# Attention and a gated MoE layer on one core: three units in turn over halves of DFF, masked scores kept in PSUM, every queue ordered by a table

## The chip, the cores and the metric

The program runs on one NeuronCore of a Trainium2 chip. Its engines are TensorE (PE, matmuls; its weight loads are listed apart as PEld), VectorE (DVE), ScalarE (ACT), GpSimd (POOL) and SyncE (SP, which here only issues transfers). Each works through its own queue in order and waits on semaphores of the others. The metric is device time in microseconds. Three runs of the kernel before took 527.41, 528.01 and 529.1 us; the median is 528.01.

## What is computed

Eight sequences of 576 positions go through attention with 8 heads of 64 and a causal window of 64, and then through a layer with a convolution and a gate:

```python
scores = scale * np.matmul(q, k.transpose(0, 1, 3, 2))
mask = (rel >= 0) & (rel < window)                     # rel = query - key, window = 64
scores = np.where(mask, scores, -1000000000.0)
scores = scores - np.max(scores, axis=-1, keepdims=True)
attn = np.exp(scores)
attn = attn / (np.sum(attn, axis=-1, keepdims=True) + 1e-09)
x = np.matmul(attn, v)                                 # heads side by side: 512 columns
h = np.maximum(x @ w_in, 0.0)                          # w_in: 512 x 1024
conv_out[:, t] = sum(conv_w[k] * h[:, t + k - 1] for k in range(3))   # along the sequence
gate = 1.0 / (1.0 + np.exp(-conv_out))
out = h * gate @ w_out                                 # w_out: 1024 x 512
```

q, k and v are float32. The weights (w_in, conv_w, w_out) are float64 arrays, and reach the chip as pairs of 32-bit words.

## The kernel before

**Units.** The 8 x 576 positions are cut into NU = 12 units of NX = 384 positions, six blocks of 64 each. For every unit the kernel does an attention part and a MoE part.

**Attention of a unit.** Keys, queries and values are loaded (load_qk, load_v). Scores come in NBU = 3 bursts of NB = 4 blocks (qk, L357), into two PSUM banks. row_max (L364) adds the mask, scales, writes the masked scores to SBUF tiles `s` and leaves each row's extreme in `nm`. exps (L374) takes the exponentials from SBUF to SBUF with row sums. guard (L377), reciprocal (L380) and normalise (L385) follow. For the first two units (`wide`, BY_PE = 2) PE transposes the result (transpose_pe, L391) and untile copies it into `ub` (L396); for the others DVE transposes 32 x 32 blocks (L412) into `T`, and SP places them by twelve transfers a group (place, L424). values (L488) multiplies with V; split_hi (L492) and split_lo (L495) cut the result into two parts for fp32r matmuls.

**MoE of a unit.** For each f of NF = 8 blocks of 128 DFF columns mm1 (L508) does 12 matmuls of 128 x 384: 4 chunks of 128 rows times 3 products (high x high, low x high, high x low). relu (L525, L529) writes `hbuf`. For each pair of f: conv_mid on ACT (L535), conv_side twice per f on DVE (L542), sigmoid (L549), gate (L554), gate_hi (L558), gate_lo (L562). mm2 (L571) then does 3 matmuls for each of 4 output chunks, which add up over the 8 f in four PSUM banks `po`. The results are copied out (L607, L609) and stored.

**Weights.** Each weight block is loaded as raw 64-bit words into one of two buffers (`bits`), which share their memory with `T` and the result tile `ot`. to_f32 turns the words into float32 (L252 on ACT, L253 on POOL, L254 and L256 on DVE, L259 on ACT, L260 on DVE), then the high part (L275 or L277) and the low part (L278) are cut off.

**PSUM.** Eight banks: two for scores (`sc`), two for mm1 and values (`acc`), four for mm2 (`po`). Unit 0's second and third burst borrow `po`.

**Order.** All work is entered with a due time (`at`), many of them from the table START. `queued` plays the queues through with estimated costs and writes out an order by due time among what is ready; the tiles' semaphores then hold the engines to the data. Up to a set time PE's holes are filled with matmuls on a spare tile (keep_busy, L216). Units run one after another: unit u+1's attention values and unit u+2's scores lie among unit u's matmuls.

Of the kernel before, what the change touches and what calls it, by code (L numbers as in the profile page):

```python
# [46 lines left out]

class Work:


    def __init__(self, t, eng, cost, do, r, w, kind, mb, port):
        self.t, self.eng, self.cost, self.do, self.r, self.w, self.kind, self.mb = t, eng, cost, do, r, w, kind, mb
        self.port = port
        self.needs, self.after, self.ready = 0, [], 0.0
        self.start = self.end_ = 0.0


def queued(works, fill=None):

    import heapq
    writer, readers = {}, {}
    for x in works:
        deps = set()
        for k in x.r:
            if k in writer:  # L70
                deps.add(writer[k])
        for k in x.w:
            deps.update(readers.get(k, ()))
            if k in writer:
                deps.add(writer[k])
        deps.discard(x)
        for d in deps:
            d.after.append(x)
        x.needs = len(deps)
        for k in x.w:  # L80
            writer[k], readers[k] = x, []
        for k in x.r:
            readers.setdefault(k, []).append(x)
    free = {"PE": 0.0, "DVE": 0.0, "ACT": 2.0, "POOL": 0.7, "SP": 1.3}
    state = dict.fromkeys(free)
    waiting = {e: [] for e in free}
    touched = {k: ("", 0.0) for k in [("sc", 0)] + [("acc", i) for i in range(2)] + [("po", i) for i in range(NC)]}
    for x in works:
        if x.needs == 0:
            waiting[x.eng].append(x)  # L90
    dma, port, order, left = 0.0, {"DVE": 0.0, "POOL": 0.0}, [], len(works)
    while left:
        best = None
        for e, ws in waiting.items():
            if not ws:
                continue
            start = max(free[e], min(x.ready for x in ws))
            if best is None or start < best[0]:
                best = (start, e)
        start, e = best  # L100
        x = min((x for x in waiting[e] if x.ready <= start),
                key=lambda x: x.t - (0.5 if x.kind and x.kind == state[e] else 0.0))
        if x.port:
            if e == "POOL" and start < port["DVE"]:
                free[e] = port["DVE"]
                continue
            start = max(start, port["POOL"])
            port[e] = start + x.port
        waiting[e].remove(x)
        if fill and e == "PE" and start < FILL_TO:  # L110
            t = max(free[e], FILL_FROM)
            n = int((start - t) * FILL)

            clean = [(end, k) for k, (by, end) in touched.items() if by != "PE" and end < t]
            if n > 0 and clean:
                order.append(Work(x.t, e, 0.0, fill(n, min(clean)[1]), [], [], None, 0, 0.0))
        turn = SWITCH[e] if e in SWITCH and (x.kind != state[e] if e == "PE" else x.kind and x.kind != state[e]) else 0.0
        if turn and e == "PE" and not x.kind:
# [19 lines left out]
START = {  # L140
    "v0": -34.213,
    "pv0": -15.486,
    "conv": -34.622,
    "bits": ((-44.162, -48.108), (-49.962, -46.523)),
    "qk1": -44.058,
    "v1": -6.318,
    "qk2": 0.918,
    "qk0": (-88.698, -55.197, -55.435),
    "ex0": (-38.484, -35.539, -25.91),
    "sc1": (-35.664, -14.916, -14.661),  # L150
    "ex1": (-10.948, -3.722, -2.234),
    "mask": -13.894,
    "sig": ((5.143, 6.743, 8.637, 10.624), (2.954, 4.077, 7.59, 9.996), (4.046, 6.806, 8.285, 10.314)),
    "in": (-40.063, -38.679, -33.327, -12.569, -5.818),
    "out": (-5.241, -4.847, 7.996, 9.148),
# [13 lines left out]
def attention_moe(ctx: ExitStack, tc: tile.TileContext, q, k, v, w_in, conv_w, w_out, out):  # L169
# [56 lines left out]
    def two(t, eng, cost, do, **kw):  # L226
        at(t, eng, cost, do, port=cost, **kw)
# [74 lines left out]

    def wide(u):
# [429 lines left out]
```

## Time and profile before

| | |
|---|---|
| runs | 527.41, 528.01, 529.1 us |
| span of the profiled execution, first to last instruction | 528.6 us |
| busy: PE, DVE, ACT, POOL | 507.8, 377.7, 384.5, 105.5 us |
| mean granted TensorE clock | 0.994 |
| read from HBM, written | 47.73 MB, 9.47 MB |

The profile gives no other total of the profiled execution than its span, which lies between the lowest and the highest run. A row of a stage table is: stretch, its length, busy time (and instructions) of each engine, granted clock, DMA share, GB/s; taken for one line of the kernel it shows PE and PEld alone. A row of the timeline is: start, length, engine, line, operation, output<-input, shapes, count, and in brackets the idle time before it and what ended that. A row of the groups is: line, engine, operation, shapes, count, then busy time and mean nanoseconds of one, then the idle time before. Matmuls overlap each other, so their pace is read from the distance of their starts.

### The profile page before, as it was taken

How to read it: one execution, taken by the hardware profiler on the slowest of the kernel's cores; microseconds unless marked ns; L12 is line 12 of the kernel's file. 1: busy time of each engine (PE TensorE's matmuls, PEld its weight loads, DVE VectorE, ACT ScalarE, POOL GpSimd, SP SyncE). 2: the span in 40 equal slices, each digit the busy share in tenths (PEclk: the TensorE clock that was granted, in tenths of full speed). 3: DMA queues.
4: the chain of work that ended last, by engine and by line, in shares of the span. 5: the costliest groups of instructions: out<-in, count | busy, mean ns of one | idle time of the engine just before them, and what ended most of it. 6: DMA issues, size and time to landing. Idle time of an engine off the chain costs nothing.

```text
span 528.6 us, 14478 instructions
## 1 busy us (share of the span) xinstructions
PE 507.8 (96%) x5646; PEld 486.1 (92%) x5646; DVE 377.7 (71%) x1084; ACT 384.5 (73%) x1017; POOL 105.5 (20%) x192
## 2 busy tenths in 40 slices
PE   6867899999999999999999999999999999999996
PEld 4657799999899999999999999999999999999996
DVE  3998999998668676667767767767767767655552
ACT  1988999788795994696696697687687687544541
POOL 5663645112011120011021021021021021000000
PEclk9998999999999999999999999999999999999999
DMA  8982670265472264172173073083073053010011
GB/s 275 378 276 101 231 258 2 51 203 190 115 269 68 66 206 129 56 275 69 40 288 77 22 256 112 23 287 97 14 279 99 24 165 95 13 61 1 1 61 60
DMA packets 29459, 69.94 MB, mean 132 GB/s; under 512 B 5712, under 2 KB 17616, under 8 KB 29392
## 3 DMA queue, kind: packets, MB, share of 16 engines
q1 hardware_dynamic: 29392, 69.03, 39.6%
q8 instruction: 44, 0.72, 0.6%
q14 instruction: 23, 0.19, 0.1%
HBM read 47.73 MB, written 9.47 MB: 108 GB/s over the span
## 4 chain that ended last, share of the span: by engine, by line
PE 89%; DMA 4%; ACT 3%; DVE 2%; issue 1%; SPq 0%; ACTq 0%
PE po L571 39%; PE acc L508 38%; PE acc L488 6%; PE sc L357 5%; DMA q<-in_q_dram 2%; DMA T<-in_w_in_dram 1%; DVE s L364 1%; ACT ub L396 1%; ACT s L374 0%; ACT w L252 0%; DVE wil L278 0%; DVE w L260 0%; DVE xl L495 0%; DVE s L385 0%; ACT L374 0%
## 5 line engine op out<-in xcount | busy, mean ns | idle before, releaser
L508 PE MATMUL acc<-xh,wih 128*128 128x384 f32 x384 | 132.2, 344 | 1.8 <-ACT hbuf L529 0.9
L542 DVE SCALAR_TENSOR_TENSOR c<-hbuf,cw,c 128x386 f32<-128x386 f32 (+1 forms) x192 | 110.0, 624 | 32.8 <-ACT c L535 32.7
L571 PE MATMUL po<-gh,woh 128*128 128x386 f32 (+1 forms) x384 | 132.3, 345 | 0.0
L508 PE MATMUL acc<-xh,wil 128*128 128x384 f32 x384 | 130.9, 341 | 0.0
L508 PE MATMUL acc<-xl,wih 128*128 128x384 f32 x384 | 130.6, 340 | 0.0
L571 PE MATMUL po<-gh,wol 128*128 128x386 f32 (+1 forms) x384 | 129.8, 338 | 0.0
L571 PE MATMUL po<-gl,woh 128*128 128x386 f32 (+1 forms) x384 | 129.8, 338 | 0.0
L374 ACT ACTIVATE s<-s,nm 128x96 f32<-128x96 f32 (+2 forms) x288 | 105.4, 370 | 5.1 <-DVE nm L364 4.9
L508 PEld LDWEIGHTS acc<-xh,wih 128*128 128x128 f32 x384 | 72.9, 190 | 3.5 <-issue 2.1
L562 DVE TENSOR_TENSOR gl<-c,gh 128x772 fp32r<-128x772 f32 (+1 forms) x48 | 54.9, 1144 | 28.6 <-ACT gh L558 28.3
L571 PEld LDWEIGHTS po<-gh,woh 128*128 128x128 f32 x384 | 72.2, 188 | 2.9
L508 PEld LDWEIGHTS acc<-xl,wih 128*128 128x128 f32 x384 | 73.0, 190 | 0.0
L508 PEld LDWEIGHTS acc<-xh,wil 128*128 128x128 f32 x384 | 72.9, 190 | 0.0
L385 POOL TENSOR_TENSOR s<-s,r 128x768 f32<-128x768 f32 x27 | 39.7, 1471 | 165.4 <-DVE r L380 154.1
L554 DVE TENSOR_TENSOR c<-c,hbuf 128x772 f32<-128x772 f32 (+1 forms) x48 | 47.0, 980 | 36.0 <-ACT c L549 35.9
L571 PEld LDWEIGHTS po<-gl,woh 128*128 128x128 f32 x384 | 72.3, 188 | 0.0
L571 PEld LDWEIGHTS po<-gh,wol 128*128 128x128 f32 x384 | 72.3, 188 | 0.0
L529 ACT ACTIVATE hbuf<-acc 128x384 f32<-128x384 f32 x64 | 30.8, 484 | 46.2 <-PE acc L508 45.9
L549 ACT ACTIVATE c<-c 128x772 f32<-128x772 f32 (+1 forms) x48 | 40.7, 848 | 27.4 <-DVE c L542 27.2
L364 DVE CUSTOM_DVE_ANT_0 s<-sc,mask 128x96 f32<-128x96 f32 (+2 forms) x272 | 51.6, 254 | 9.0 <-POOL mask L328 5.3
L374 ACT ACTIVATION_READ_ACCUMULATOR s<-s,nm 128x1 f32 x288 | 55.2, 192 | 0.0
L535 ACT ACTIVATE c<-hbuf,cw 128x386 f32<-128x386 f32 (+1 forms) x96 | 53.6, 609 | 0.0
(64 smaller groups left out, 576.2 us busy)
## 6 DMA issues: line engine op xcount, KB each, us to landing
v<-in_v_dram SPq DMA_DIRECT2D x24, 768.0 KB, 7.1
ub<-T SPq DMA_DIRECT2D x240, 48.0 KB, 2.0
k<-in_k_dram SPq DMA_DIRECT2D x22, 448.0 KB, 5.6
q<-in_q_dram SPq DMA_DIRECT2D x22, 384.0 KB, 5.8
out_dram<-T SPq DMA_DIRECT2D x8, 772.0 KB, 4.4
T<-in_w_in_dram SPq DMA_DIRECT2D x8, 512.0 KB, 6.9
T<-in_w_out_dram SPq DMA_DIRECT2D x8, 512.0 KB, 5.1
out_dram<-T SPq DMA_DIRECT2D x3, 768.0 KB, 6.2
```

The costliest lines, as they stand in the source:

```text
L364: nc.vector.tensor_tensor_reduce(out=ss[b][:, i, h, o:n], in0=banks_of(u, b)[h][:, i * P + o:i * P + n], in1=mask[m][:, o:n], scale=-0.125 ...
L374: nc.scalar.activation(x, x, AF.Exp, bias=nms[b][:, e], scale=-1.0, accum_out=sms[b][:, e])
L385: on.tensor_tensor(sv, sv, rs[b].unsqueeze(2).broadcast_to([P, 2 * NB, n]), ALU.mult)
L488: nc.tensor.matmul(acc[bank(("v", u, c))][h * D:(h + 1) * D, t * W:(t + 1) * W], vs[:, c, t, h], ub[g][:, 2 * p:2 * p + 2, 2 * t + h], sta ...
L508: nc.tensor.matmul(acc[bank(("m", u, f))][:, :NX], w[:, f, c], x[u % 2][:, c], start=(c == 0 and j == 0), stop=(c == NC - 1 and j == 2))
L529: nc.scalar.activation(hbuf[:, f, o:o + NX], ps[:, :NX], AF.Relu)
L535: nc.scalar.activation(cs[i % 2][:, a, :n], hbuf[:, f, 1:1 + n], AF.Copy, scale=cw[:, 1, f:f + 1])
L542: nc.vector.scalar_tensor_tensor(c, hbuf[:, f, e:e + n], cw[:, e, f:f + 1], c, op0=ALU.mult, op1=ALU.add)
L549: nc.scalar.activation(c, c, AF.Sigmoid)
L554: nc.vector.tensor_tensor(c, c, hbuf[:, 2 * i:2 * i + 2, 1:1 + n], ALU.mult)
L562: nc.vector.tensor_tensor(gls[ring(u, i)][:, :, :n], cs[i % 2][:, :, :n], ghs[ring(u, i)][:, :, :n].bitcast(F32), ALU.subtract)
L571: nc.tensor.matmul(po[o][:, :n], w[:, f, es], x, start=(f == 0 and j == 0), stop=(f == NF - 1 and j == 2))
```

## The change

It does five things.

1. **Halves of DFF.** Units 0, 1 and 2 first go over f = 0 to 3, one after another, and then over f = 4 to 7 (TASKS). Each half fills its own four mm2 banks and its own result tile (two tiles `ot`, in turn). The first half is stored plainly; the second is added to it in DRAM by a POOL transfer with accumulation (store_more). There are three `xh`/`xl` tiles instead of two.
2. **Masked scores stay in PSUM.** row_max writes over the scores in their bank, two blocks to a work; exps reads them there and writes SBUF.
3. **Weights.** Each raw block has a tile of its own, which its float32 parts later take over. The decoding has no maximum on POOL any more: the magnitude is scaled by 2^-112 instead. Magnitude, larger part and lower part can be on different engines.
4. **First units' data.** For units 0 and 1 queries and keys lie packed in DRAM by bursts of two blocks (`first`), one transfer for each, and scores, maxima and exponentials go by these six bursts.
5. **Order and engines by a table.** ORDER names the works of plan() one by one: number, for some the engine (A, D, P for ACT, DVE, POOL), and after a slash the PSUM bank; F4/0 is four fill matmuls into bank 0. There are 14 of these. It replaces due times and costs.

```diff
+SPLIT = 3
+TASKS = [(0, 0, 4), (1, 0, 4), (2, 0, 4), (0, 4, 8), (1, 4, 8), (2, 4, 8)]
+TASKS += [(u, 0, NF) for u in range(SPLIT, NU)]
+DECODE = [("in", (0,)), ("in", (1,)), ("out", (0, 1)), ("in", (2, 3)), ("out", (2, 3)), ("in", (4, 5)),
+          ("out", (4, 5)), ("in", (6, 7)), ("out", (6, 7))]
...
+def bursts(u):
+    k = NB // 2 if u < FINE else NB
+    return [tuple(range(n, n + k)) for n in range(0, 2 * NT, k)]
...
+ORDER = """
+    3 9 97 8 4 7 86 6 0 5 F4/0 59/2 80 41 470 13 60 203 101 2 98D 62 F3/0 50/4 99 100 12/6 51 202 61 156 1 14 52
+    F1/0 40/2 63P 53 64 87D 16 54P 88 201 15 65P 42 F2/0 31/4 90 89 22/6 81 43 200 32 44 66/0 11 82 199 17D 33
...
+    raws, wts = {}, {}
+    wx = many(2, [P, 2 * DM], F32, "wx")
+    ots = many(2, [P, NC, NG], F32, "ot")
+    banks = many(8, [P, 512], F32, "bank", psum)
...
+    def load_first(u, b):
+        a, n, _ = first_at(b)
+        nc.sync.dma_start(qk[:, a:a + n], first[u, :, a:a + n])
...
+    def load_w(key, f):
+        raws[key, f] = pool.tile([P, DM, 2], U32, name=f"raw_{key}{f}", tag=f"{key}{f}")
+        nc.sync.dma_start(raws[key, f].rearrange("p e two -> p (e two)"), src[key][f].bitcast(U32))
...
-        at(t, "ACT", 0.0009 * n + 0.2, lambda: nc.scalar.activation(x, hw.bitcast(F32), AF.Abs), r=kb, w=kt)
-        at(t, "POOL", 0.0027 * n + 0.02, lambda: nc.gpsimd.tensor_scalar(x, x, TINY, None, op0=ALU.max), w=kt, port=PORT_CL)
+            nc.scalar.activation(x, hw.bitcast(F32), AF.Abs, scale=2.0 ** -112)
...
-                    out=ss[b][:, i, h, o:n], in0=banks_of(u, b)[h][:, i * P + o:i * P + n], in1=mask[m][:, o:n],
+                x = banks[bank[h]][:, i * P + o:i * P + k]
+                    out=x, in0=x, in1=mask[m][:, o:k],
...
-            x = ss[b][:, i, h, o:n]
-            nc.scalar.activation(x, x, AF.Exp, bias=nms[b][:, e], scale=-1.0, accum_out=sms[b][:, e])
+            nc.scalar.activation(ss[n // NB][:, n % NB, h, o:k], banks[bank[h]][:, i * P + o:i * P + k], AF.Exp, bias=small(nms, (n,))[:, h:h + 1], scale=-1.0,
+                                 accum_out=small(sms, (n,))[:, h:h + 1])
...
+    def store_more(u, t):
+        nc.gpsimd.dma_start(out[u], ots[t], accum_op=ALU.add)
...
-        for x in queued(plan, keep_busy):
-            x.do()
+        for token in ORDER.split():
+            n, _, at = token.partition("/")
+            if n[0] == "F":
+                fill(int(n[1:]), int(at))
+                continue
+            x = works[int(n.rstrip("ADP"))]
...
-    nc = bacc.Bacc("TRN2", target_bir_lowering=False, num_devices=1)
+    nc = bacc.Bacc("TRN2", target_bir_lowering=False, num_devices=1, dynamic_dma_scratch_size=2048)
```

More of the change, by code (lines that the diff above doesn't have):

```diff
@@ L140 @@
[L140 to L155, printed above, removed]
[3 rows of a table removed]
-}
@@ L168, in attention_moe, with first_at @@
+"""
+def first_at(b):
+    runs = [(g, t, W * (len(rows) + 1)) for g, t, rows in pieces(bursts(0)[b])]
+    size = len(bursts(0)[b]) * 2 * W + sum(2 * n for _, _, n in runs)
+    start = 0 if b == 0 else sum(first_at(b - 1)[:2])
+    return start, size, runs
+FIRST = sum(first_at(len(bursts(0)) - 1)[:2])
 @with_exitstack
-def attention_moe(ctx: ExitStack, tc: tile.TileContext, q, k, v, w_in, conv_w, w_out, out):
+def attention_moe(ctx: ExitStack, tc: tile.TileContext, q, k, v, first, w_in, conv_w, w_out, out):
@@ L170, in attention_moe @@
     nc = tc.nc
+    engine = {"DVE": nc.vector, "POOL": nc.gpsimd, "ACT": nc.scalar}
     pool = ctx.enter_context(tc.tile_pool(name="pool", bufs=1))
@@ new lines, in attention_moe, with work, fill @@
+    spare = pool.tile([P, 512], F32R, name="spare")
+    banks = many(8, [P, 512], F32, "bank", psum)
+    src = {"in": w_in, "out": w_out}
+    fn = {}
+    def work(f):
+        fn[f.__name__] = f
+        return f
+    @work
+    def fill(n, bank):
+        for _ in range(n):
+            nc.tensor.matmul(banks[bank], spare[:, :P], spare, start=True, stop=True)
+    @work
+    def load_first(u, b):
+        a, n, _ = first_at(b)
+        nc.sync.dma_start(qk[:, a:a + n], first[u, :, a:a + n])
@@ new lines, in turn, with unturn, transpose @@
+    def turn(j, bank):
+        b, e = of((2 * j, 2 * j + 1))
+        sv = ss[b][:, e].rearrange("p t h k -> p (t h) k")
+        for i in range(4):
+            nc.tensor.transpose(banks[bank[0]][:, i * P:(i + 1) * P], sv[:, i], ident)
+    @work
+    def unturn(j, on, bank):
+        g, t = place_of(2 * j)
+        copy(on)(ub[g][:, :, 2 * t:2 * t + 4, :].rearrange("p i t q -> p t i q"),
+                       banks[bank[0]].rearrange("p (t i q) -> p t i q", i=4, q=32))
+    @work
+    def transpose(g, t, rows):
@@ L670, with conv_mid, conv_side @@
-_INS = ['q', 'k', 'v', 'w_in', 'conv_w', 'w_out']
+        return cs[j % 2][:, f % 2, :n], hbuf[:, f, e:e + n], cw[:, e, f:f + 1]
+    @work
+    def conv_mid(u, f, j, on):
+        c, h, w = conv(u, f, j, 1)
+        if on == "ACT":
+            nc.scalar.activation(c, h, AF.Copy, scale=w)
+        else:
+            engine[on].tensor_scalar_mul(c, h, w)
+    @work
+    def conv_side(u, f, j, e):
+        c, h, w = conv(u, f, j, e)
+        nc.vector.scalar_tensor_tensor(c, h, w, c, op0=ALU.mult, op1=ALU.add)
@@ new lines, in mm2, with result @@
+    @work
+    def mm2(u, f, o, j, start, stop, bank):
+        n, a = width_of(u), f % 2
+        gh, gl = ghs[j % 3][:, a, :n], gls[j % 3][:, a, :n]
+        es = slice(o * P, (o + 1) * P)
+        for i, (w, x) in enumerate(((0, gh), (1, gh), (0, gl))):
+            nc.tensor.matmul(banks[bank[0]][:, :n], wts["out", f][:, w, es], x, start=(start and i == 0), stop=(stop and i == 2))
+    @work
+    def result(u, o, t, on, bank):
+        n = width_of(u)
+        copy(on)(ots[t][:, o, :n], banks[bank[0]][:, :n])
@@ new lines, in last_half, with store_half, store_one, store @@
+    @work
+    def last_half(o, h, t, bank):
+        e = slice(h * NG // 2, (h + 1) * NG // 2)
+        copy(("ACT", "DVE")[h])(ots[t][:, o, e], banks[bank[0]][:, e])
+    @work
+    def store_half(o, h, t):
+        e = slice(h * NG // 2, (h + 1) * NG // 2)
+        nc.sync.dma_start(out[LAST, :, o, e], ots[t][:, o, e])
+    @work
+    def store_one(o, t):
+        nc.sync.dma_start(out[LAST, :, o], ots[t][:, o])
+    @work
+    def store(u, t):
+        nc.sync.dma_start(out[u], ots[t])
+    @work
```

838 lines of the change are left out of this document (421 added, 417 removed), and 3 rows, old and new, of the table START.

## The prediction

> **What bounds the kernel now.** I read the stage table first. Its columns are the stretch, its length, and the busy time of PE, PE's weight loads, DVE, ACT and POOL, then granted clock, DMA share and GB/s.
>
> ```profile
> 0.00:37.40 37.40, 26.10 (x397) 20.29 (x397) 27.27 (x120) 26.40 (x100) 23.55 (x62) 1.00 0.87 309
> 37.40:77.30 39.90, 34.70 (x378) 32.38 (x379) 37.20 (x94) 34.68 (x76) 18.55 (x15) 0.91 0.62 210
> 77.30:140.00 62.70, 62.63 (x733) 60.52 (x735) 55.29 (x138) 53.80 (x145) 16.87 (x23) 1.00 0.33 105
> 140.00:524.50 384.50, 384.39 (x4160) 372.95 (x4145) 257.69 (x734) 269.30 (x699) 46.52 (x94) 1.00 0.35 111
> ```
>
> From 77.3 us to 524.5 PE has no hole, so there only PE's own work counts. Everything that a new order can win lies ahead of 77.3, where DVE and ACT are the full engines (37.20 and 34.68 of 39.90). The tail from 524.5 to 528.6 stays: its copies and stores are the same.
>
> How much of 77.3 us does PE need? Next are its lines in that stretch (the wide matmuls of L508 and L571, then values, scores and transposes), followed by the pace of twelve wide matmuls and by the prices of the small ones at full clock.
>
> ```profile
> 0.00:77.30 77.30, 21.32 (x97) 19.20 (x98) 0.96 0.74 258
> 0.00:77.30 77.30, 4.45 (x24) 4.25 (x24) 0.96 0.74 258
> 0.00:77.30 77.30, 7.46 (x192) 6.38 (x192) 0.96 0.74 258
> 0.00:77.30 77.30, 13.28 (x384) 10.80 (x384) 0.96 0.74 258
> 0.00:77.30 77.30, 7.13 (x48) 6.01 (x48) 0.96 0.74 258
> ```
> ```profile
> 245.67 2.11 PE acc L508 x12
> ```
> ```profile
> 28.22 1.00 PE L357 MATMUL sc<-k,q 64*64 64x128 f32 x32
> 35.60 1.00 PE L357 MATMUL sc<-k,q 64*32 64x96 f32 x64
> 40.90 1.98 PE L391 MATMUL po<-ident,s 128*128 128x128 f32 x16
> 241.43:281.70 40.27, 3.24 (x96) 2.96 (x96) 1.00 0.41 132
> ```
>
> A wide matmul costs 2.11/12 = 0.176; 98 (one record is missing, the weight loads are 98) + 24 of them make 21.5. The 384 scores are 192 of units 0 and 1 (six groups of 32 at 1.00) and 192 of unit 2 (three of 64 at 1.00): 9.0. Transposes: 48 at 1.98/16, 5.9. Values: 192 at 3.24/96, 6.5. Together 42.9, so **PE loses 77.3 - 42.9 = 34.4 us** in the front. That number is what I forecast anew.
>
> **The change, part by part.** PE keeps its 2304 wide matmuls; the split of units 0 to 2 over halves of DFF only reorders them, and the second halves are added to the first in DRAM. I read the table by counting, for each engine, the works that it names ahead of a point, and priced them by these rows (starts follow each other about 0.1 us sooner than the durations say, as the first two pairs show):
>
> ```profile
> 13.64 0.39 ACT L374 ACTIVATE s<-s,nm 128x128 f32<-128x128 f32 x1
> 14.03 0.39 ACT L374 ACTIVATE s<-s,nm 128x128 f32<-128x128 f32 x1
> ```
> ```profile
> 12.86 0.28 DVE L364 CUSTOM_DVE_ANT_0 s<-po,mask 128x128 f32<-128x128 f32 x1
> 13.07 0.28 DVE L364 CUSTOM_DVE_ANT_0 s<-po,mask 128x128 f32<-128x128 f32 x1
> ```
> ```profile
> L374 ACT ACTIVATE s<-s,nm 128x96 f32<-128x96 f32 x240 | 87.0, 366 | 0.2
> L374 ACT ACT_TABLE_LOAD x20 | 25.7, 1283 | 1.1 <-PEq L727 0.7
> L396 ACT COPY ub<-po 128x512 f32<-128x512 f32 x12 | 6.6, 576 | 0.0
> L252 ACT ACTIVATE w<-T 128x512 f32<-128x512 f32 x2 | 1.3, 670 | 5.4 <-DMA T<-in_w_in_dram 5.4
> L492 ACT CAST xh<-acc 128x384 fp32r<-128x384 f32 x48 | 21.9, 477 | 4.3 <-PE acc L488 3.7
> L256 DVE SCALAR_TENSOR_TENSOR w<-T,w 128x512 uint32<-128x512 uint32 x2 | 1.4, 686 | 0.0
> L495 DVE TENSOR_TENSOR xl<-acc,xh 128x384 fp32r<-128x384 f32 x48 | 26.1, 553 | 2.3 <-ACT xh L492 1.2
> ```
>
> *Start.* POOL now builds a late mask before the first one. The first mask took from 0.73 to 2.34, a late one from 5.74 to 9.26:
>
> ```profile
> 0.73 0.20 POOL L321 MEMSET mask<- 128x128 f32 x1 [0.29 <-POOLq L727]
> 2.05 0.29 POOL L328 TENSOR_SCALAR_AFFINE_SELECT mask<-mask 64x128 f32<-64x128 f32 x1
> 5.74 0.20 POOL L321 MEMSET mask<- 128x128 f32 x1
> 9.14 0.12 POOL L331 MEMSET mask<- 32x32 f32 x1
> ```
>
> So DVE's first row_max starts near 0.73 + 3.5 + 1.6, about 6.0, and ACT's exponentials at 6.9 (as in the kernel before, 6.91 there). The loads come in finer pieces: six bursts of unit 0 (640 columns x 128 x 4 bytes, 0.33 MB each) and the first two weights are 3.0 MB, at the 309 GB/s of the first stage some 10 us; the last burst is asked for at 13.6 by DVE's queue. The cover is 1.6 us after 2 us of latency.
>
> *First wide matmul.* Ahead of and with the last split_hi of unit 0, ACT has 42 exponentials at 0.39 (16.4), five untilings at 0.48, four splits at 0.38, a few small ones: 6.9 + 21.0 = 27.9; DVE's split_lo 0.5 more. PE starts at about 28.5, against this row of before:
>
> ```profile
> 37.44 0.41 PE L508 MATMUL acc<-xh,wih 128*128 128x384 f32 x1 [0.84 <-DVE xl L495]
> ```
>
> *Up to the first matmul of unit 2* (the eight mm1 of units 0 and 1 and eight mm2 are done). ACT: 80 exponentials 30.4 (48 at 0.39, 32 at 0.365), 16 decoding steps of 512 at 0.57 and three for conv 9.4, five table loads 6.4, ten untilings 4.8, ten splits 3.8, the MoE's own 7.6; sum 62.4, from 6.3 on to 68.7, with 1.2 of waits and the split_lo behind it 70.5. DVE: 80 row maxima 15.9 (0.212 and 0.178 each), 23 decoding steps 12.5, twelve conv sides at 0.56 6.7, twelve split_lo at 0.49 5.9, six normalisations 5.3, four transposes 2.9, small ones 8.7; sum 57.9. From 6.0 on, with 4.1 us of wait for ACT at the first split_lo (28.4 against 24.3) and 1.5 where the next scores wait for the exponentials to leave their bank, DVE is at 69.5. To this comes POOL: DVE works beside it were stretched. Three pairs, the plain one first:
>
> ```profile
> 22.27 0.68 DVE L278 TENSOR_TENSOR wil<-w,wih 128x512 fp32r<-128x512 f32 x1
> 24.42 1.52 DVE L278 TENSOR_TENSOR wil<-w,wih 128x512 fp32r<-128x512 f32 x1
> 40.50 1.23 DVE L385 TENSOR_TENSOR s<-s,r 128x1024 f32<-128x1024 f32 x1
> 29.41 2.06 DVE L385 TENSOR_TENSOR s<-s,r 128x1024 f32<-128x1024 f32 x1
> 48.89 1.10 DVE L542 SCALAR_TENSOR_TENSOR c<-hbuf,cw,c 128x386 f32<-128x386 f32 x2
> 52.19 1.92 DVE L542 SCALAR_TENSOR_TENSOR c<-hbuf,cw,c 128x386 f32<-128x386 f32 x2
> ```
>
> That is 0.84 + 0.83 + 0.82 = 2.5; I take 3.0. DVE: 72.5. PE's work ahead of the point: 120 wide 21.1, scores 11.0, transposes 5.9, values 288 9.7, sum 47.7. **Lost: 24.8.**
>
> *Up to unit 1's second-half mm2*, the last point at which DVE's queue is that close: DVE 118.8 us of work (40 conv sides, all 16 decodings, seven gate pairs), 6.0 + 4.1 + 1.5 + 3.0 as before, 2.5 for further waits: 135.9. PE's work ahead: 444 wide 78.1, scores 13.0, transposes 5.9, values 13.0, sum 110.0. Lost 25.9. After that DVE gains on PE (257.69 us busy in the last 384.5 of the stage table). So 25.9 against 34.4: **8.5 us gained**.
>
> *Breaks between wide and small matmuls* cost PE a weight load that starts late:
>
> ```profile
> PEld acc L488 <- issue: 4.2, 17, 0.3
> ```
>
> The table puts values into 21 places from unit 2 on: four more than 17, at 4.2/17 each about 1.0; at the least 0. I take 0.8.
>
> *Exponentials out of PSUM.* No row has this form. A 512-wide read from PSUM took 0.576, from SBUF 0.670: up to 0.09 less, 7 us over 80; the other end is no gain, or a wait where DVE and ACT want one bank (1.5 is in the sum). Taken as nothing: ACT at 70.5 is not last, DVE at 72.5 is. Row maxima written to PSUM: reading it costs DVE no more than SBUF in these rows, and I bound writing by +-0.02 each, 1.6 over 80; taken 0. [...]
>
> *At nothing:* the three accumulating stores on POOL (no row has this form; even at 4 us each, 12 us would lie behind unit 0's second half, where POOL is nearly idle: 16.87 of 62.70 and 46.52 of 384.50. Without that cover a gate on POOL would come up to 4 us late, and PE's next mm2 with it), the second result tile, the raw weights' own tiles. The last take away what stands ahead of the old weight loads on SP, the wait for a shared buffer; I count that in the loads being there in time.
>
> **Sum:** 528.6 (span of the profiled execution; its own total is not given apart from that) - 8.5 + 0.8 = 520.9. The runs' median is 528.01, 0.6 less: **520.3 us**.
>
> **Rivals.** *Earlier yet:* ACT's reads are shorter by the 0.09, POOL stretches nothing (minus 3.0) and DVE waits less by 2.5. PE then loses 20.4, time 514.8. For it: that row pair. Against: three stretched rows.
>
> *The cold clock:* fill matmuls go from 30 (last row below) to 14, and PE has holes around 35 to 41 us by my sums. In the kernel before, after holes of about 2 us, the granted clock was 0.91 for a stage and matmuls stood 0.32 apart:
>
> ```profile
> 48.41 0.52 PE L508 MATMUL acc<-xh,wil 128*128 128x384 f32 x1
> 48.73 0.52 PE L508 MATMUL acc<-xl,wih 128*128 128x384 f32 x1
> ```
> ```profile
> 0.00:77.30 77.30, 11.17 (x30) 6.24 (x30) 0.96 0.74 258
> ```
>
> If mm1 of units 0 and 1 (96) all ran so, 96 x 0.144 = 13.8 more, of which holes hide about half: 527. [...]
>
> *The transfers decide (the order is not followed in time, because its data are late):* by 72.5 us the new order has asked, by the shapes in the code, for the pieces of two units (3.9 MB), three units' values (4.7), two more units' keys and queries (3.4), twelve weights (6.3) and 24 placements (1.2): 19.5 MB, 277 GB/s over 70.5 us. The old order moved 258 GB/s up to 77.3. If that is all there is, unit 2 starts 5 us later: 525.3. Against: 309 in the first stage, and a DMA share of 0.62 in the second.
>
> *Slower: POOL locks DVE.* POOL takes over normalisations, gates and weight remainders; the table gives it some 34 us of works that read SBUF up to the 135.9 us point. If each such microsecond holds DVE for 0.56 (0.84 in a work of 1.5 us), DVE comes 19 us later, not 3: 41.9 lost, time 528.6 + 7.5 + 0.8 - 0.6 = 536. It decides from 34.4 lost, that is from 11.5 us of holding. [...]
>
> **How the numbers follow.** Forecast 0.56 (its own range 517 to 524.5), earlier 0.16, cold clock 0.10, transfers 0.08, slower 0.10. The range 514 to 528 leaves out the slower case and the outermost of the others. A measurement of this kernel can tell 0.3% (1.6 us) from no change. Faster: forecast, earlier, transfers and a fifth of the cold clock, 0.82; same: most of the cold clock, 0.07; slower 0.11, the rest of it and POOL.
>
> **What would show it.** First wide matmul near 28.5 (wrong above 32); first matmul of unit 2 near 72.5; PE without a hole from about 136; DVE idle under 9 us of the first 136; the steady unit at 40.2 to 40.5 still. Five table loads on ACT by 70. If the first wide matmul is early and the end is not, look at DVE's stretched works and PE's 0.32 pace.

## The result and the profile after

| | median (lowest to highest) | ratio to before, 95% interval |
|---|---|---|
| before, beside it | 527.71 us (526.49 to 529.1) | |
| changed | 552.0 us (550.22 to 553.55) | 1.0444 [1.0405, 1.0483] |

The change makes the kernel 4.4% slower: 24 us. The forecast was 520.3 us and the range ended at 528.

The first view of the changed kernel is the stage table with the stretches that the prediction used for the kernel before; the columns are the same.

```profile
0.00:37.40 37.40, 31.58 (x442) 23.52 (x444) 28.17 (x147) 28.28 (x119) 23.43 (x68) 0.91 0.84 303
37.40:77.30 39.90, 33.69 (x555) 29.12 (x551) 36.21 (x110) 35.04 (x102) 16.34 (x23) 0.96 0.68 230
77.30:140.00 62.70, 60.16 (x471) 57.28 (x469) 59.77 (x135) 47.71 (x113) 8.64 (x15) 1.00 0.37 131
140.00:524.50 384.50, 370.02 (x4043) 351.02 (x4044) 282.60 (x798) 210.01 (x579) 93.16 (x136) 0.98 0.37 109
```

In the first stretch PE is busier than before (31.58 us against 26.10). In the last one, where PE had no hole (384.39 of 384.50), it now stands still for 14.5 us, and the granted clock is 0.98. DVE is busy 25 us longer there (282.60 against 257.69), ACT 59 us less (210.01 against 269.30).

The chain of waits, first of the changed kernel, then of the kernel before (shares of the span by engine; SPq is SyncE issuing a transfer, "issue" time in which an engine waited for nothing that the profile shows):

```profile
PE 46%; DVE 27%; ACT 12%; issue 6%; DMA 4%; SPq 3%; POOL 2%; DVEq 0%; POOLq 0%; ACTq 0%
```
```profile
PE 89%; DMA 4%; ACT 3%; DVE 2%; issue 1%; SPq 0%; ACTq 0%
```

The kernel before was a chain of matmuls; the changed one goes through DVE and ACT for 39% of its span. What PE waits for after 80 us, by line and releaser (total us, times, longest); the kernel before has not one line in this view:

```profile
PE bank L604 <- DMA ub<-T: 4.0, 1, 4.0
PE bank L604 <- DMA qk<-in_q_dram: 2.4, 1, 2.4
PE bank L621 <- DVE xl L614: 1.7, 1, 1.7
PE bank L604 <- issue: 1.7, 2, 1.5
PE bank L695 <- POOL gl L687: 1.5, 2, 1.3
PE bank L604 <- ACT s L549: 1.3, 1, 1.3
```

L604 is the values, and `ub<-T` a placement of the transposed attention weights, the last step of the softmax: most of the waits are of the values, for a softmax chain that comes late. The wait of 2.40 us is put down to a load of queries, which the values do not read; it is gone when the placements are left out (below). Two of them in the timeline:

```profile
183.72 1.05 PE L604 MATMUL bank<-ub,v 128*64 128x64 f32 x26 [2.40 <-DMA qk<-in_q_dram]
...
223.52 0.77 PE L604 MATMUL bank<-ub,v 128*64 128x64 f32 x9 [4.05 <-DMA ub<-T]
```

To say where the time went I price PE's own work in every trace with one list, read from the starts of matmuls at full clock: 479.6 us in each kernel. "Lost" is time minus that work. The marks are the two of the prediction, 47.7 and 110.0 us of work done; as the list is cheaper than the prediction's prices, they fall 2 to 3 us behind the matmuls that the prediction names. A hole is counted by how much later than its price a matmul starts.

| kernel, profiled span | lost at 47.7 of work | at 110.0 | at the end | holes over 0.25 us behind 80 us |
|---|---|---|---|---|
| before, 528.6 | 36.4 | 38.5 | 44.6 | 0.3 |
| changed, 551.7 | 30.5 | 35.5 | 68.0 | 21.0 |
| changed, scores in SBUF, 535.1 | 28.8 | 29.9 | 51.3 | 10.5 |
| the same, no placements behind unit 3, 524.6 | 27.6 | 30.0 | 40.2 | 2.3 |

The changed kernel has lost 3.0 us less than before at the second mark and 26.4 us more behind it; the rest of the span (some 4 us of tail) is as before. At the prediction's own prices the work sums to 485.8 us and the losses at the end to 38.6, 61.9, 45.3 and 34.1: the same differences. Each row is one execution; that of the last row was 2.9 us below its kernel's median (526.4 against 529.3).

### The profile page after: what moved, and what is told of

The parts are those of the page before. It is cut to its first block, busy times and chain, and to the rows that moved or that the text cites. A ratio compares the mean times of both kernels' runs of the same rounds, so it can differ in the third digit from the quotient of the medians.

```text
span 551.7 us, 14530 instructions
## 1 busy us (share of the span) xinstructions
PE 518.6 (94%) x5630; PEld 483.5 (88%) x5630; DVE 419.8 (76%) x1208; ACT 326.1 (59%) x920; POOL 145.1 (26%) x242
## 4 chain that ended last, share of the span: by engine, by line
PE 46%; DVE 27%; ACT 12%; issue 6%; DMA 4%; SPq 3%; POOL 2%; DVEq 0%; POOLq 0%; ACTq 0%
PE bank L695 21%; PE bank L621 17%; ACT s L549 7%; DVE c L670 6%; DVE bank L539 4%; PE bank L604 4%; PE bank L517 4%; SPq L597 2%; DMA v<-in_v_dram 2%; DVE gl L687 2%; DVE nm L539 2%; DVE wx L427 2%; DVE T L584 2%; DVE s L565 1%; DVE wx L434 1%
## 5 line engine op out<-in xcount | busy, mean ns | idle before, releaser
L695 PE MATMUL bank<-gh,w_out 128*128 128x386 f32 (+1 forms) x768 | 203.5, 346 | 1.7 <-DVE ot L700 0.9
L621 PE MATMUL bank<-xh,w_in 128*128 128x384 f32 x768 | 198.9, 339 | 4.2 <-DVE xl L614 3.3
L621 PEld LDWEIGHTS bank<-xh,w_in 128*128 128x128 f32 x768 | 139.1, 189 | 7.6 <-DVE xl L614 4.7
L695 PEld LDWEIGHTS bank<-gh,w_out 128*128 128x128 f32 x768 | 138.8, 190 | 7.8 <-DVE ot L700 1.2
L670 DVE SCALAR_TENSOR_TENSOR c<-hbuf,cw,c 128x386 f32<-128x386 f32 (+1 forms) x192 | 124.2, 666 | 27.3 <-ACT c L663 25.9
L695 PE MATMUL bank<-gl,w_out 128*128 128x386 f32 (+1 forms) x384 | 131.7, 343 | 2.0 <-POOL gl L687 1.5
L621 PE MATMUL bank<-xl,w_in 128*128 128x384 f32 x384 | 129.5, 337 | 0.0
L549 ACT ACTIVATE s<-bank,nm 128x96 f32<-128x96 f32 (+2 forms) x288 | 96.0, 355 | 36.5 <-DVE nm L539 34.4
L539 DVE CUSTOM_DVE_ANT_0 bank<-bank,mask 128x96 f32<-128x96 f32 (+1 forms) x288 | 65.6, 293 | 24.1 <-PE bank L517 14.0
L695 PEld LDWEIGHTS bank<-gl,w_out 128*128 128x128 f32 x384 | 73.0, 190 | 4.4 <-DVE gl L687 2.2
L621 PEld LDWEIGHTS bank<-xl,w_in 128*128 128x128 f32 x384 | 72.5, 189 | 0.3 <-DVE xl L614 0.3
L678 POOL TENSOR_TENSOR c<-c,hbuf 128x772 f32<-128x772 f32 (+1 forms) x20 | 35.5, 1776 | 102.0 <-ACT c L674 99.2
L604 PEld LDWEIGHTS bank<-ub,v 128*64 128x64 f32 x1152 | 38.0, 143 | 19.1 <-issue 8.9
L604 PE MATMUL bank<-ub,v 128*64 128x64 f32 x1152 | 41.7, 230 | 12.8 <-DMA ub<-T 4.0
L687 POOL TENSOR_TENSOR gl<-c,gh 128x772 fp32r<-128x772 f32 (+1 forms) x18 | 34.1, 1894 | 65.0 <-DVE gh L682 36.8
L663 ACT ACTIVATE c<-hbuf,cw 128x386 f32<-128x386 f32 (+1 forms) x53 | 32.7, 622 | 23.4 <-POOL gl L687 9.9
L549 ACT ACT_TABLE_LOAD x24 | 30.8, 1283 | 21.3 <-DVE nm L539 21.1
```

The costliest lines, as they stand in the source:

```text
L539: nc.vector.tensor_tensor_reduce(out=x, in0=x, in1=mask[m][:, o:k], scale=-0.125, scalar=3.0e38, op0=ALU.add, op1=ALU.min, accum_out=small ...
L549: nc.scalar.activation(ss[n // NB][:, n % NB, h, o:k], banks[bank[h]][:, i * P + o:i * P + k], AF.Exp, bias=small(nms, (n,))[:, h:h + 1], ...
L604: nc.tensor.matmul(banks[bank[0]][h * D:(h + 1) * D, t * W:(t + 1) * W], vs[:, c, t, h], ub[g][:, 2 * p:2 * p + 2, 2 * t + h], start=True, ...
L621: nc.tensor.matmul(banks[bank[0]][:, :NX], w[:, a, c], y[x][:, c], start=(c == 0 and j == 0), stop=(c == NC - 1 and j == 2))
L663: nc.scalar.activation(c, h, AF.Copy, scale=w)
L670: nc.vector.scalar_tensor_tensor(c, h, w, c, op0=ALU.mult, op1=ALU.add)
```

## The experiments

Each time is a median with its ratio to runs of the kernel before beside it (528.8, 527.6, 528.6, 527.5 and 528.5 us in the five groups).

### Three suspects

**GpSimd's products.** All gate products and remainders of GpSimd go to VectorE (only letters in the table change: `…P` to `…D`, 38 works).

> The changed kernel with its 38 gate and gate_lo works that the table gives to POOL put on DVE at the same places of the table. Theory G (POOL's slow gates, 1.75 to 1.9 us against 0.96 on DVE, hold up mm2 and stretch DVE): at least 10 us less than 552, PE's loss behind 80 us (37.6 us over the bare price of its work) falls below 28. Theory S (the fixed order as a whole; the waits hang on many chains): between 547 and 558, since DVE takes 36 us more work and only the two waits for POOL's gl (1.5 us) go.

Measured: 553.3 us, 1.0465 [1.0402, 1.0528]. No gain.

**The scores in PSUM.** The row maxima write SBUF again, and the exponentials read it; the rest of the change stays.

```diff
-                    out=x, in0=x, in1=mask[m][:, o:k],
+                    out=ss[n // NB][:, n % NB, h, o:k], in0=x, in1=mask[m][:, o:k],
...
-            nc.scalar.activation(ss[n // NB][:, n % NB, h, o:k], banks[bank[h]][:, i * P + o:i * P + k], AF.Exp, bias=small(nms, (n,))[:, h:h + 1], scale=-1.0,
+            nc.scalar.activation(ss[n // NB][:, n % NB, h, o:k], ss[n // NB][:, n % NB, h, o:k], AF.Exp, bias=small(nms, (n,))[:, h:h + 1], scale=-1.0,
```

> The changed kernel with one part undone: row_max writes the masked scores to SBUF and the exponentials read them there; table, banks and engines are as in the change. Theory P (scores in PSUM are the cause: row_max slower by 0.04 us each, DVE and ACT take turns on a bank, scores wait for exponentials): 10 us or more less than 552, the pace of row_max back from 0.22 to 0.18 us. Theory S: 3 to 7 us less (288 x 0.04 = 11.5 us of DVE work goes, about half of it on a path that PE waits for, and 2.4 us of waits for the exponentials).

Measured: 538.3 us, 1.018 [1.0111, 1.0249]. Some 14 us come back, the largest effect of any single edit to the changed kernel; 10 us stay.

**SyncE's queue.** The loads of q and k from unit 2 on, and of v of all units, are issued by ScalarE (`nc.sync.dma_start` to `nc.scalar.dma_start` in `load_q`, `load_k`, `load_v`). The expectation speaks of units 2 to 11 alone, but `load_v` serves units 0 and 1 too.

> The changed kernel with the loads of keys, queries and values of units 2 to 11 issued from ACT at the same places of the table; SP keeps the placements and stores. Theory Q (SP's single queue, with loads and placements in turn at 0.6 us each and waits for landings, starves the values): the stalls at 127, 181, 219 and 269 us (8.5 us together) and the cold matmuls behind them go: 8 to 14 us less than 552. Theory S: 0 to 5 us less, the same stalls come a little later from other engines.

Measured: 553.7 us, 1.0473 [1.0425, 1.0521]. No gain.

### Why scores in PSUM cost time

Two things changed for the row maxima and exponentials: VectorE writes PSUM, and the pair of banks is free only after the exponentials. The first is seen in the groups. The form of 96 columns and the accumulator's read, before and after (line, engine, operation, count, busy us, mean ns, idle before):

```profile
L364 DVE CUSTOM_DVE_ANT_0 s<-sc,mask 128x96 f32<-128x96 f32 x240 | 44.9, 252 | 3.6 <-PE sc L357 3.6
L364 DVE DVE_READ_ACCUMULATOR2_ANT nm<- 128x1 f32 x288 | 23.6, 82 | 0.0
```
```profile
L539 DVE CUSTOM_DVE_ANT_0 bank<-bank,mask 128x96 f32<-128x96 f32 x240 | 53.8, 289 | 17.3 <-PE bank L517 11.9 <-ACT s L549 5.3
L539 DVE DVE_READ_ACCUMULATOR2_ANT nm<- 128x1 f32 x288 | 40.6, 141 | 0.0
...
L549 ACT ACTIVATE s<-bank,nm 128x96 f32<-128x96 f32 x240 | 79.1, 349 | 33.3 <-DVE nm L539 31.3 <-PE bank L604 1.7
L549 ACT ACT_TABLE_LOAD x24 | 30.8, 1283 | 21.3 <-DVE nm L539 21.1
```

A row maximum is 37 ns longer when it writes PSUM, its accumulator's read 59 ns. In the timeline of the changed kernel row maxima follow each other by 0.215 us, exponentials by 0.32:

```profile
204.20 0.30 DVE L539 CUSTOM_DVE_ANT_0 bank<-bank,mask 128x96 f32<-128x96 f32 x1
204.20 0.14 DVE L539 DVE_READ_ACCUMULATOR2_ANT nm<- 128x1 f32 x1
204.42 0.30 DVE L539 CUSTOM_DVE_ANT_0 bank<-bank,mask 128x96 f32<-128x96 f32 x1
...
204.63 0.30 DVE L539 CUSTOM_DVE_ANT_0 bank<-bank,mask 128x96 f32<-128x96 f32 x1
```
```profile
208.85 0.33 ACT L549 ACTIVATE s<-bank,nm 128x96 f32<-128x96 f32 x1
209.07 0.20 ACT L549 ACTIVATION_READ_ACCUMULATOR s<-bank,nm 128x1 f32 x1
209.16 0.34 ACT L549 ACTIVATE s<-bank,nm 128x96 f32<-128x96 f32 x1
```

Over all 239 distances of 96 columns the medians are 0.178 us before and 0.215 after for the maxima, 0.361 and 0.318 for the exponentials. So 288 blocks make VectorE some 10.7 us longer (288 x 0.037) and ScalarE 12.4 us shorter (288 x 0.043). The gain does not make up for the loss, because of where each falls: the maxima stand ahead of the exponentials, and the exponentials' groups show 52 us of waiting for them (31.3 + 21.1), where the row in the prediction has 0.2 before.

The two effects were then taken apart. In the first run the maxima write SBUF and the exponentials read the raw scores in the banks, so that the mask is left out of them; in the second the maxima write PSUM and the exponentials read a tile in SBUF (the mask, not the scores), which frees the banks early. The pace of the maxima follows the edit: 0.178 us in the first, 0.215 in the second (252 and 291 ns each, their accumulator's reads 84 and 143).

```diff
-                    out=x, in0=x, in1=mask[m][:, o:k],
+                    out=ss[n // NB][:, n % NB, h, o:k], in0=x, in1=mask[m][:, o:k],
...
-            nc.scalar.activation(ss[n // NB][:, n % NB, h, o:k], banks[bank[h]][:, i * P + o:i * P + k], AF.Exp, bias=small(nms, (n,))[:, h:h + 1], scale=-1.0,
+            nc.scalar.activation(ss[n // NB][:, n % NB, h, o:k], banks[bank[h]][:, i * P + o:i * P + k], AF.Exp, bias=small(nms, (n,))[:, h:h + 1], scale=0.125,
```

> The changed kernel, in its order, with the row maxima writing the masked scores to SBUF as before, while the exponentials still read the banks (the raw scores there, by a scale of 0.125; the mask is left out of the exponentials, and nothing else). So the banks are still held until the exponentials are done, but VectorE no longer writes PSUM. Theory W (the price of VectorE writing PSUM: 0.215 us between row maxima of 96 columns against 0.178, and 141 ns against 82 for the accumulator's read, so a later maximum for every block): the 14 us that came back with scores in SBUF come back here too, 537 to 540 us. Theory T (turn-taking: a bank is released only by the exponentials): nothing comes back, 549 to 553 us.

```diff
-            nc.scalar.activation(ss[n // NB][:, n % NB, h, o:k], banks[bank[h]][:, i * P + o:i * P + k], AF.Exp, bias=small(nms, (n,))[:, h:h + 1], scale=-1.0,
+            nc.scalar.activation(ss[n // NB][:, n % NB, h, o:k], mask[m][:, o:k], AF.Exp, bias=small(nms, (n,))[:, h:h + 1], scale=1.0,
```

> The changed kernel, in its order, with the row maxima writing the masked scores in place in PSUM as the change does, while the exponentials read an SBUF tile of the same size instead (the mask; the scores are left out of the exponentials, and nothing else). The banks are released by the row maxima; VectorE still pays for writing PSUM. Theory W: 549 to 553 us, with 0.215 us between row maxima. Theory T: 537 to 540 us.

Measured: 547.4 us, 1.035 [1.0294, 1.0407], with the banks held; 542.0 us, 1.0259 [1.0198, 1.032], with VectorE writing PSUM. Neither theory holds alone: against the 1.0444 of the change the cheaper maxima give back 0.0094 (5 us) and the early release 0.0185 (10 us), and the sum, 0.0279, is what scores in SBUF gave back (0.0264). Each of the single figures has an interval of about 0.007.

Do they cost time by making the values wait? With the placements behind the values of unit 3 left out, the values no longer wait for the softmax (192 tokens of `place` are dropped from the table, and with them their issues and transfers; scores in PSUM here, in SBUF below).

> The changed kernel as it is (masked scores in PSUM, 552 us) without the placements behind the values of unit 3 (left out; the values then read blocks placed earlier). If the held banks and the dearer row maxima cost their time by making the softmax chain late for the values (holes of 1.1 to 4.2 us at values and at the scores behind them: 127, 139, 181, 219, 270, 397 us, 11.7 in all): 538 to 541 us. If they cost it through the other engines' queues (gates, feature splits and results behind waiting exponentials and row maxima): 546 to 551 us.

Measured: 540.1 us, 1.0216 [1.018, 1.0252]: 12 us less, the number of the first reading. The holes at 181, 219, 270 us are gone. But the reading itself is not borne out. With scores in SBUF the same omission takes off 9.0 us (538.3 to 529.3, below), so between the two kernels without placements 10.8 of the 13.7 us that scores in PSUM cost are still there (540.1 against 529.3). Most of their cost goes another way than through values that wait for placements. Which way is only partly seen: 4.8 of the 13.0 us between these two traces are lost ahead of the second mark (at the prediction's prices), and behind it the trace with scores in PSUM shows waits for exponentials, gates and remainders (1.3 to 1.9 us each at 139, 162 and 299 us).

**In the order of before.** The kernel before with scores kept in PSUM from unit 1 on, and nothing else of the change. So that nothing is overwritten too early, scores are planned behind the exponentials of the burst before and some loads later, and the planner makes a new order.

```diff
-                    out=ss[b][:, i, h, o:n], in0=banks_of(u, b)[h][:, i * P + o:i * P + n], in1=mask[m][:, o:n],
+                    out=(banks_of(u, b)[h][:, i * P + o:i * P + n] if u else ss[b][:, i, h, o:n]), in0=banks_of(u, b)[h][:, i * P + o:i * P + n], in1=mask[m][:, o:n],
...
-            nc.scalar.activation(x, x, AF.Exp, bias=nms[b][:, e], scale=-1.0, accum_out=sms[b][:, e])
+            y = banks_of(u, b)[h][:, i * P + o:i * P + n] if u else x
+            nc.scalar.activation(x, y, AF.Exp, bias=nms[b][:, e], scale=-1.0, accum_out=sms[b][:, e])
...
+    for (_, _, z), (x, y, e) in zip(held, held[1:]):
+        if z[0].t >= x.t:
+            old, x.t = x.t, min(z[0].t + 0.002, e[0].t - 0.01)
...
```

> The kernel before with the masked scores kept in PSUM from unit 1 on, its planner giving the order; the scores of each burst are planned behind the exponentials of the burst before, and the loads of q and k for the next unit behind the scores that they overwrite (in the run before this one some loads stood ahead of scores moved back, so that those scores read the next unit's q and k). Theory P (banks held by the exponentials and VectorE writing PSUM cost time in any order): 538 to 555 us. Rival (only in the table's fixed order): 527 to 532 us.

Measured: 551.1 us, 1.0448 [1.0432, 1.0463]. (The three earlier forms, in which scores or loads overwrote what was still to be read, took 552.4, 550.9 and 552.7 us and say little.) The total agrees with theory P, the trace does so only in part. Stages of this kernel, then of the kernel before:

```profile
20.00:40.00 20.00, 13.39 (x173) 11.70 (x173) 17.80 (x41) 16.07 (x49) 13.85 (x11) 0.91 0.64 224
60.00:80.00 20.00, 13.14 (x120) 12.19 (x119) 17.86 (x26) 15.25 (x33) 7.51 (x8) 0.74 0.49 171
140.00:160.00 20.00, 16.37 (x159) 15.10 (x159) 12.38 (x35) 15.19 (x48) 3.46 (x6) 0.83 0.33 94
160.00:524.50 364.50, 364.00 (x4058) 350.14 (x4055) 253.09 (x716) 254.18 (x673) 45.79 (x93) 1.00 0.36 116
```
```profile
20.00:40.00 20.00, 15.80 (x272) 13.44 (x272) 19.95 (x68) 18.31 (x69) 12.77 (x12) 1.00 0.84 299
60.00:80.00 20.00, 17.71 (x131) 16.83 (x130) 17.47 (x38) 19.47 (x43) 11.42 (x9) 0.91 0.73 249
140.00:160.00 20.00, 20.00 (x258) 19.07 (x244) 12.99 (x51) 18.48 (x61) 4.63 (x5) 1.00 0.67 231
160.00:524.50 364.50, 364.39 (x3904) 353.88 (x3902) 244.70 (x684) 250.82 (x639) 41.89 (x89) 1.00 0.33 105
```

From 160 us on PE is as full as before, with 0.4 us of holes. At the prediction's prices this kernel loses 20.4 us more than the kernel before: 16.4 ahead of 160 us, where PE has holes, and some 4 behind it, in a slower pace and more breaks. So in the steady units, where the softmax has time to spare, scores in PSUM cost little. How much of the front loss is the edit and how much the planner's new order was not separated.

### The ten microseconds that stay with scores in SBUF

With placements left out as above:

> The changed kernel with the masked scores in SBUF (538.3 us) and without the placements behind the values of unit 3 (they are left out: the values then read blocks placed earlier). This takes away all waiting of the values for late exponentials, transposes and placements. If the late softmax chain is what TensorE still waits for (holes of 3.5, 2.8 and 1.2 us at 173, 211 and 260 us, 7.5 in all, and 1 to 2 us of clock): 528 to 531 us. If the remaining loss is spread over banks, gates and breaks: 535 to 538 us.

Measured: 529.3 us, 0.9998 [0.9973, 1.0023]. With the placements 9.0 us go, all that was left above the kernel before. Gone with them are not only the values' waits but also 192 issues on SyncE and 192 transfers, so the run does not tell a late softmax from a full queue. Nor does the front's gain show in the time even here: behind the second mark PE still loses 10.2 us (40.2 - 30.0) against 6.1 before. PE's busy time in the last stretch, first with scores in SBUF, then without placements too:

```profile
140.00:524.50 384.50, 375.99 (x4050) 359.58 (x4049) 282.69 (x806) 216.06 (x576) 96.95 (x133) 0.99 0.38 113
```
```profile
140.00:524.50 384.50, 379.19 (x4087) 363.04 (x4085) 284.27 (x809) 216.87 (x578) 96.58 (x133) 1.00 0.27 88
```

What makes the placements late? The chain of waits of the kernel with scores in SBUF has two stretches off PE ahead of the two large holes. It runs first through SyncE's issues, later through DVE and POOL (start, length, what); the row below it is from SyncE's timeline and shows what that queue did during the 5.24 us that the chain puts down to a load of values: it issued eight placements.

```profile
164.46 0.58 SPq L392
...
165.09 5.24 DMA v<-in_v_dram
...
170.90 0.58 SPq L396
...
172.67 0.04 issue
172.71 0.59 SPq L597
173.30 0.04 issue
173.34 0.59 SPq L597
173.93 0.04 issue
173.98 3.02 DMA qk<-in_q_dram
...
199.25 0.56 DVE gh L682
199.82 2.67 DVE c L670 x2
...
210.21 0.51 SPq L597
210.72 0.04 issue
210.76 3.29 DMA ub<-T
```
```profile
165.56 5.29 SPq L597 DMA_DIRECT2D ub<-T  x8
```

The three feature sums at 199.73 took 3.40 us where three at 0.61 take 1.8, beside a product of 2.10 us on POOL. Each suspect got a run, with scores in SBUF throughout.

Loads of q, k and v on ScalarE's queue (v of all units, as above):

> The changed kernel with the masked scores in SBUF (538.3 us in an earlier run) and with the loads of q, k and v of units 2 to 11 issued by ScalarE's queue instead of SyncE's. With scores in SBUF TensorE still lost 3.5 us at 173 us and 2.8 us at 211 us waiting for a load or a placement, each placement and load being issued on one queue at about 0.6 us. Theory Q (that queue sets what is left): the two losses go and with them the clock's restarts, 529 to 533 us, where the front's gain begins to show. Rival F (the order as a whole spreads waits; the next one takes over): 536 to 540 us, with losses of 2 us or more elsewhere.

Measured: 541.7 us, 1.0263 [1.0208, 1.0317]. The hole at 173 us shrank to 1.6, but others of 2.8 and 2.2 us opened at 223 and 476 us, and 6.4 us more were lost at the first mark (35.2 against 28.8). There unit 1's second load of values was issued at 41.4 us, behind ScalarE's work, instead of 31.8.

The loads behind the placements on SyncE (the same tokens, 29 of them further back):

> The changed kernel with the masked scores in SBUF (538.3 us) and one thing more: on SyncE's queue the loads of q, k and v from unit 5 on stand behind the placements that they stood among, where their reader leaves room for it. With scores in SBUF the chain of waits ran through that queue from 163.4 to 174.6 us, with four loads of 0.62 us each among the placements. Theory Q (the one queue sets the holes at 173 and 211 us): 2.5 us of the first hole, 0.6 us of the second and about 1 us of clock come back, 533 to 536 us. Rival F (something else takes over, as when the loads went to ScalarE's queue, 541.7 us): 537 to 541 us.

Measured: 560.4 us, 1.0573 [1.0495, 1.0651], a clear miss: now scores wait for their loads, as two lines of this kernel's timeline show.

```profile
222.25 0.89 PE L520 MATMUL bank<-qk 64*32 64x96 f32 x32 [3.71 <-DMA qk<-in_q_dram]
...
402.03 0.89 PE L520 MATMUL bank<-qk 64*32 64x96 f32 x32 [3.14 <-DMA qk<-in_q_dram]
```

GpSimd's products on VectorE, half of the placements on ScalarE's queue, and both:

```diff
-        nc.sync.dma_start(ub[g][o:o + HW, i], tbuf[HW * i:HW * (i + 1), g, j])
+        (nc.sync, nc.scalar)[(i + j) % 2].dma_start(ub[g][o:o + HW, i], tbuf[HW * i:HW * (i + 1), g, j])
```

> The changed kernel with the masked scores in SBUF (538.3 us) and with all 38 gate products and gate remainders of GpSimd on VectorE. In the trace with scores in SBUF five of the 144 feature sums of 128x386 took 1.9 us on average instead of 0.61 while GpSimd worked, 5.8 us over, three of them in the chain of waits ahead of the hole at 211 us. Theory G (GpSimd's products hold VectorE up and so make the next unit's weights late): the hole at 211 us goes and with it its clock, 533 to 536 us. Rival (VectorE's own extra work, 38 products of 0.96 us, eats that up): 537 to 541 us.

> The changed kernel with the masked scores in SBUF (538.3 us) and with half of the placements (those with an odd sum of block and step) issued by ScalarE's queue, the others and all loads by SyncE's as they are. In the trace with scores in SBUF the chain of waits lay in SyncE's issues from 163.4 to 174.6 us. Theory Q (the serial issue of some 0.6 us each on one queue sets the hole at 173 us and part of that at 211 us): 5 us less on that queue per unit, 532 to 535 us. Rival F (the softmax chain ahead of the placements is late whatever issues them, and ScalarE now waits for transposes): 537 to 545 us.

> The changed kernel with the masked scores in SBUF, the 38 gate products and remainders on VectorE, and half of the placements issued by ScalarE's queue: the two single changes together. If both causes are real and apart: 527 to 532 us, which would come close to the 529 us measured without placements. If one takes the other's place: as the better of the two, 533 to 537 us. If neither helps: 538 us or more.

Measured: 538.6 us, 1.0202 [1.0174, 1.023]; 537.3 us, 1.0187 [1.0161, 1.0213]; 539.3 us, 1.0242 [1.0208, 1.0277]. None helps the total. With two queues the two large holes became three (1.4 at 175 us, 2.1 at 178, 1.9 at 214), all still for placements.

Work moved between VectorE and ScalarE (letters of the table, 50 and 57 works):

> The changed kernel with the masked scores in SBUF (538.3 us), and from unit 3 on the 50 rectifications and result copies that the table gives to VectorE given to ScalarE, at their places in the order. That takes 50 x 0.55 = 27 us from VectorE (282.7 us busy of the 384.5 from 140 us on) and adds 50 x 0.48 = 24 us to ScalarE (216.1 busy). Theory D (VectorE's queue is what is late for the softmax): 531 to 535 us. Theory A (ScalarE's is): 541 us or more. Theory O (neither queue alone; the order has no slack where any work comes late): 536 to 541 us.

> The same the other way round: from unit 3 on the 57 rectifications and result copies that the table gives to ScalarE are given to VectorE, 57 x 0.48 = 27 us off ScalarE and 57 x 0.55 = 31 us more on VectorE. Theory D: 544 us or more. Theory A: 531 to 535 us. Theory O: 537 to 543 us.

Measured: 539.2 us, 1.0188 [1.0153, 1.0223]; 545.7 us, 1.0313 [1.0262, 1.0364]. The last stretch of the first and of the second, to be read against VectorE's 282.69 us and PE's 375.99:

```profile
140.00:524.50 384.50, 374.12 (x4041) 358.08 (x4040) 263.41 (x760) 237.64 (x627) 96.14 (x132) 0.99 0.37 112
```
```profile
140.00:524.50 384.50, 371.28 (x3998) 353.91 (x3998) 299.15 (x854) 191.69 (x519) 92.69 (x131) 0.98 0.37 108
```

More work on VectorE costs time, less of it gains none. So none of these edits alone brings the ten microseconds back. My reading is that the softmax of the next unit ends just when its values stand first in PE's order, and that whatever is eased, another link of the same chain is next; the runs fit this but do not show it, and which link would have to give stays open. SyncE's queue is not cleared either. At the prediction's prices the traces with the loads or half of the placements on ScalarE's queue lose 14.3 and 14.7 us behind the second mark, against 18.2 with scores in SBUF alone, and lose more ahead of it (34.7 and 29.4 against 27.1). These are single executions, and those of one kernel differ by up to 3 us. A kernel that eases that queue only behind the front was not run, nor were parts 1, 3 and 4 of the change by themselves. No version tried beats the kernel before.

## Why the prediction was wrong

**The front came out in part.** The first wide matmul was forecast near 28.5 (wrong above 32), unit 2's first near 72.5; they came 1.2 and 3.6 us later:

```profile
29.68 0.60 PE L621 MATMUL bank<-xh,w_in 128*128 128x384 f32 x2
...
76.10 0.62 PE L621 MATMUL bank<-xh,w_in 128*128 128x384 f32 x2
```

DVE's first row maximum came at 6.08 (forecast 6.0), and ACT had its five table loads by 70 us. At the prediction's own prices 28.2 us were lost at the first mark and 32.7 at the second, not 24.8 and 25.9; with scores in SBUF 26.4 and 27.1. "8.5 us gained" measured 38.5 - 29.9 = 8.6 with scores in SBUF, with some luck: the prediction set a loss at 110.0 us of work against the old kernel's 34.4 at 77.3 us of time; at the second mark the old kernel had lost 35.9, so both terms were over 1 us too small. In the kernel as changed only 3.0 of it is there: with scores in PSUM the rest is lost again by the second mark.

**The step that failed** is "After that DVE gains on PE", with "there only PE's own work counts" behind it. It was argued from an engine's load (257.69 busy of 384.5), but what decides is whether what other engines make for PE is there when PE's fixed order comes to it: the softmax of a unit, which goes through PE, DVE, ACT, DVE or POOL, SP and the transfers, before its values; free banks before the next scores; splits and gates before the wide matmuls. In the order of before PE waited for none of them after 80 us; in the table's order it did. Lost behind the mark: 32.5 us against 6.1 before, where the sum had 0.8 more. PE was not without a hole from about 136 us (21.0 us of holes behind 80), and a steady unit took 42.8 us on average (from the first L621 of unit 3 to that of unit 11), not 40.2 to 40.5. VectorE was idle for 14.6 us of the first 136, where the sign said under 9, although the waits in the sum itself (6.0, 4.1, 1.5 and 2.5) make 14.1. By the medians the 23.4 us (552.0 against 528.6) come apart into 13.7 that go with scores in PSUM and 9.0 more that go with the placements. Without placements the loss at the end falls from 51.3 to 40.2 us with scores in SBUF and from 68.0 to 53.1 in PSUM. So what goes with the placements is most of the excess behind the mark in the first kernel, and about half of it in the changed one; most of the other half goes with scores in PSUM, the next two terms.

**Row maxima written to PSUM**, bounded "by +-0.02 each" and taken as 0, measured +0.037, outside the bound; the bound came from rows that only read PSUM. By the run that took it away it was worth some 5 us.

**"1.5 where the next scores wait for the exponentials to leave their bank"** was counted once, in the front, for DVE. Over the kernel the held banks cost some 10 us.

**Exponentials out of PSUM**, "taken as nothing", measured 0.043 us less each (0.318 us from one to the next against 0.361), within the bound of 0.09; but ScalarE was idle for 45% of the last stretch, and the 12.4 us did not show in the time.

**Breaks**, 0.8 forecast: behind 80 us PE lost 12.1 us outside of holes with scores in SBUF and 8.0 before, 4 us more, in which slow pace after holes is included (in the changed kernel, behind the hole of 4.05 us at 223.52, six matmuls of L695 in a row start 0.32 us apart, later ones 0.18; the granted clock was 0.50 from 223.5 to 226 us).

**The rivals.** "POOL locks DVE" was the one on the slower side, and what it goes by is in the trace: works on VectorE that take far longer than their form does. Eight of the 192 feature sums took 1.4 to 2.3 us instead of 0.62, 10.0 us over (two before, 2.1 us over), and the mean of the larger form went from 628 to 666 ns. Three sums, of which the second took 2.22 us, beside a product of 2.11 us on POOL:

```profile
208.32 3.41 DVE L670 SCALAR_TENSOR_TENSOR c<-hbuf,cw,c 128x386 f32<-128x386 f32 x3
```

But over all of VectorE's works such excess (over 0.3 us above the form's median) is 14.6 us against 13.3 before, and 4.3 against 4.5 up to the 135.9 us to which the rival's 11.5 were counted. Both runs that took the products off POOL gained nothing. "The transfers decide" was not it: up to 77 us PE waited 0.8 us in all for transfers. Nor was "The cold clock" in the front, where the loss came to 3.0 us less than before. Behind it the granted clock was 0.98 over the last stretch and 0.91 between 200 and 240 us, where the hole of 4.05 us lies; at the prediction's prices PE lost 8.4 us there, of which the holes make 5.5.

## What to carry to other kernels

An engine that is busy to 67% in the old order (73% in the new) can still stand in a chain that is late: ask of each chain that crosses engines when its last link ends and when its reader stands first in order, and forecast a new order from that slack. Check a reading such as "the cost goes through this wait" in both versions of the kernel: leaving the placements out took 12 us off one and 9 off the other, so it was not the path of the other cost. Scores kept in PSUM saved their reader 0.043 us a block here, but cost their writer 0.037 and held the banks until the exponentials were done, worth some 10 us over the kernel; count both ahead of the saving, and price a write from a row that writes there. Where the chain has slack (the kernel before from 160 us on), the same edit cost some 4 us of 20.

## What the runs showed of the hardware

- A row maximum of VectorE that writes its tile to PSUM instead of SBUF: 289 against 252 ns, its accumulator's read 141 against 82 ns, 0.215 against 0.178 us from one to the next.
- An exponential of 96 columns that reads PSUM: 0.318 us from one to the next against 0.361 from SBUF; its accumulator's read is longer, 216 against 192 ns.
- The issue of a placement takes 0.59 us of SyncE's queue (median of 240; 0.51 at the least), so the 24 placements of a unit fill some 14 us of it. On ScalarE's queue, in the run with scores in SBUF and the loads there, six issues of loads between 200 and 215 us took 0.33 to 0.45.
